# A gated stream of 64-row tiles: the first tile as two compact pieces, the larger stored first

## The chip, the cores and the metric

One core of one Trainium2 chip. The metric is device microseconds of one execution; medians of several runs are given with their range.

## The reference, cut to what matters

```python
# x: (1, 384, 384, 384) bfloat16; w1d: (1,) bfloat16
g = jnp.einsum("bhwc->bc", x) / (H * W)      # mean of every channel over 147456 pixels
s = _sigmoid(g * w1d[0])                     # k = 1: one weight
return x * s[:, None, None, :]               # every pixel times the gate of its channel
```

The gate depends on all of x, so read strictly, x would have to be read twice. The input is 113 MB; the kernel holds four tiles of 6.29 MB at a time.

## The kernel before

It guesses the gate from the first few pixels (`s_early`), multiplies and stores with that, sums everything on the way, and compares at the end the true gate with the guess, bit for bit in bfloat16. Only if a channel differs does a second pass run. So in the usual case x is read once and written once. A tile is 64 rows; a row is one pixel in each of 128 partitions, 768 bytes per partition. Four slots of 64 rows lie in SBUF. Loads go through the SP queue (some early ones through the ACT queue), stores through the ACT queue.

```python
TILE, SLOTS, EARLY, LEAD, FORE, OWN = 64, 4, 4, 8, 32, 16
PAUSE = 9
...
    def dram(view, r0, n):                    # n rows for each of 128 partitions, compact in HBM
        return view[r0 * P : (r0 + n) * P, :].rearrange("(p t) c -> p (t c)", p=P)
...
    def load(place, n, r0, queues=("sync",), lo=0, hi=None, reads=()):
        i, hi = lo, hi or n
        for queue, m in zip(queues, split(hi - lo, -(-(hi - lo) // len(queues)))):
            plan.dma(queue, at(place + i, m), dram(x_rows, r0, n)[:, i * C : (i + m) * C],
                     reads=reads, writes=rows(place + i, m))
            i += m
...
    def put(place, n, r0, to=None, parts=None):
        to, i = place if to is None else to, 0
        for m in parts or [n]:                # tile 0: two gate multiplies of 32 rows
            plan.op("vector", gate(to + i, place + i, m, s_early), ...)
            i += m
        plan.final.append(plan.dma("scalar", dram(o_rows, r0, n), at(to, n), reads=rows(to, n)))

    def pause(r0):                            # ScalarE writes row r0 of the slot: it has to wait
        to = at(base, PAUSE)                  # for the store that reads that row
        plan.op("scalar", ..., reads=["warm"], writes=rows(r0, 1) + ["pause"])
...
    load(0, TILE, 0, hi=LEAD)                                  # 8 of 64 rows: for the early gate
    plan.dma("sync", w_one[0:1, 0:1], w1d.unsqueeze(0), writes=["w_one"])
    load(0, TILE, 0, ("sync", "scalar"), lo=LEAD)              # the other 56, in two halves
    load(slot(1), TILE, row0(1))
    load(slot(2), TILE, row0(2), ("scalar", "scalar"))
    load(slot(3), TILE, row0(3))
...
    for k in range(n_tiles):
        if k >= SLOTS:
            for i in range(2) if k == SLOTS else () if k < SLOTS + 2 else (k - SLOTS,):
                sum_own(i)
                put(slot(i), TILE, row0(i), parts=None if i else (FORE, TILE - FORE))
            if k == SLOTS:
                pause(slot(k))
            load(slot(k), TILE, row0(k), reads=["pause"] if k == SLOTS else ())
```

The planner (not shown) turns reads and writes of rows into semaphore waits. The load of tile 4 goes into slot 0, so it waits for tile 0's store, and for the pause behind it.

Of the kernel before, what the change touches and what calls it, by code (L numbers as in the profile page):

```python
# [149 lines left out]
def split(n, most):  # L150
    k = -(-n // most)
    return [n // k + (i < n % k) for i in range(k)]
# [6 lines left out]
TILE, SLOTS, EARLY, LEAD, FORE, OWN = 64, 4, 4, 8, 32, 16  # L159
# [5 lines left out]
def bass_standalone__channel_attn_eca__vision_kernel(  # L165
# [8 lines left out]
    x_rows, o_rows = x.flatten_outer_dims(), out.flatten_outer_dims()  # L174

    def dram(view, r0, n):
        return view[r0 * P : (r0 + n) * P, :].rearrange("(p t) c -> p (t c)", p=P)

    ones = nc.alloc_sbuf_tensor("ones", [P, P], BF16)
    s_early = nc.alloc_sbuf_tensor("s_early", [P, C], BF16)  # L180
# [19 lines left out]
    def at(r0, n):  # L200
        assert r0 + n <= n_arena
        return arena[:, r0 * C : (r0 + n) * C]

    def rows(r0, n):
        return [("sb", r) for r in range(r0, r0 + n)]

    def gate(to, place, n, s):
        s_b = s[:].unsqueeze(1).broadcast_to([P, n, C])
        v, to_v = (at(r, n).rearrange("p (t c) -> p t c", t=n) for r in (place, to))
        return lambda e: e.tensor_tensor(to_v, v, s_b, ALU.mult)  # L210

    n_tiles = n_rows // TILE
# [3 lines left out]
    last = n_tiles - 1  # L216
    ready = nc.alloc_semaphore("ready")

    def slot(k):
        return k % SLOTS * TILE  # L220

    def row0(k):
        return k * TILE
# [2 lines left out]
    s_true = at(slot(last), 1)  # L226
    plan = Planner(nc, "a", 70)

    def load(place, n, r0, queues=("sync",), lo=0, hi=None, reads=()):

        i, hi = lo, hi or n
        for queue, m in zip(queues, split(hi - lo, -(-(hi - lo) // len(queues)))):
            plan.dma(
                queue,
                at(place + i, m),
                dram(x_rows, r0, n)[:, i * C : (i + m) * C],
                reads=reads,
                writes=rows(place + i, m),
            )
            i += m  # L240
# [90 lines left out]
    def sum_own(k):  # L331

        r0 = slot(k) + TILE - OWN
        view = at(r0, OWN).rearrange("p (t c) -> p c t", t=OWN)
        to = part if k else own
        plan.op(
            "vector",
            lambda e: e.reduce_sum(to[:], view, axis=mybir.AxisListType.X),  # L338
            reads=rows(r0, OWN),
            writes=["part" if k else "own"],  # L340
        )
        if k:
            plan.op(
                "vector",
                lambda e: e.tensor_tensor(own[:], own[:], part[:], ALU.add),  # L345
                reads=["own", "part"],
                writes=["own"],
            )
# [28 lines left out]
                writes=["acc_own"],  # L377
            )

    def put(place, n, r0, to=None, parts=None):  # L380
        to, i = place if to is None else to, 0
        for m in parts or [n]:
            plan.op(
                "vector",
                gate(to + i, place + i, m, s_early),
                reads=["s_early"] + rows(place + i, m),
                writes=rows(to + i, m),
            )
            i += m
        plan.final.append(  # L390
            plan.dma("scalar", dram(o_rows, r0, n), at(to, n), reads=rows(to, n))
        )

    def pause(r0):

        to = at(base, PAUSE)
        plan.op(
            "scalar",
            lambda e: e.activation(  # L399
                to, warm[:, 0:1].broadcast_to([P, PAUSE * C]), ACT_F.Sigmoid  # L400
            ),
            reads=["warm"],
            writes=rows(r0, 1) + ["pause"],
        )

    def weight():
# [25 lines left out]
    plan.op("gpsimd", lambda e: e.memset(warm[:, 0:1], 0.0), writes=["warm"])  # L432
    plan.op("vector", lambda e: e.memset(ones[:], 1.0), writes=["ones"])  # L433
    plan.op("gpsimd", lambda e: e.memset(zeros[:], 0.0), writes=["zeros"])
    load(0, TILE, 0, hi=LEAD)
    plan.dma("sync", w_one[0:1, 0:1], w1d.unsqueeze(0), writes=["w_one"])
    load(0, TILE, 0, ("sync", "scalar"), lo=LEAD)
    load(slot(1), TILE, row0(1))

    load(slot(2), TILE, row0(2), ("scalar", "scalar"))  # L440
# [10 lines left out]
        reads=["total", "w_scaled0", "warm1"],  # L451
        writes=["s_early"],
# [4 lines left out]
    for k in range(n_tiles):  # L457
        if k >= SLOTS:

            for i in range(2) if k == SLOTS else () if k < SLOTS + 2 else (k - SLOTS,):  # L460
                sum_own(i)
                put(slot(i), TILE, row0(i), parts=None if i else (FORE, TILE - FORE))
            if k == SLOTS:
                pause(slot(k))
            load(slot(k), TILE, row0(k), reads=["pause"] if k == SLOTS else ())
        there = rows(slot(k), TILE)
        plan.relay(ready, "gpsimd", "tensor", there, rows(slot(k), FORE), ["acc1"])
        plan.signals("tensor", rows(slot(k) + FORE, TILE - OWN - FORE), ["acc1"])
    plan.signals("tensor", [], ["acc1"])
    for k in range(n_tiles - SLOTS, last):  # L470
        sum_own(k)
        put(slot(k), TILE, row0(k))

    put(slot(last), TILE, row0(last), slot(n_tiles))
    sum_own(last)
    join_own()

# [5 lines left out]
        reads=["acc_own", "total"],  # L483
        writes=["total"],
# [6 lines left out]
        reads=["total", "w_scaled1"],  # L491
        writes=["s_true"] + rows(slot(last), 1),
# [6 lines left out]
        reads=["s_true", "s_early"],  # L499
        writes=["total"],  # L500
# [4 lines left out]
        reads=["total"],  # L505
        writes=["wrong"],
# [4 lines left out]
        reads=["wrong"],  # L511
        writes=["redo"],
# [6 lines left out]
    half, r0 = (base - above) // 2, 0  # L519
    for k, n in enumerate(split(n_rows, half)):  # L520
        place = above + k % 2 * half
# [4 lines left out]
            reads=rows(place, n),  # L526
            writes=rows(place, n),
# [98 lines left out]
```

## Time and profile before

| | before |
|---|---|
| median of 3 runs | 528.14 us (528.01 to 528.21) |
| span of the profiled run | 526.5 us |
| moved | 113.25 MB in, 113.25 MB out |
| DMA rate from 140 to 440 us | 435 GB/s |

From the timeline (start, length, engine, what), tile 0's and tile 1's store issues, and the pause:

```profile
44.14 24.76 ACTq L109 DMA_DIRECT2D out_dram<-arena  x2
76.09 3.08 ACT L399 ACTIVATE arena<-warm 128x3456 bf16<-128x3456 f32 x1 [61.87 <-DMA out_dram<-arena]
```

Two short stretches (the last column is GB/s):

```profile
1.00:10.00 9.00, 0.72 (x3) 0.20 (x2) 0.39 (x3) 1.49 (x2) 0.13 (x2) 1.00 1.02 395
50.00:57.00 7.00, 7.00 (x34) 0.00 (x0) 6.97 (x3) 0.00 (x0) 0.00 (x0) 1.00 0.98 390
```

(A stretch counts a packet whole where it starts, so stretches this short are coarse; with each packet's bytes spread over its time, the single records give 378 and 398 GB/s here.)

### The profile page before, as it was taken

What the parts mean: (1) busy time and instruction counts of PE and PEld (TensorE: products, weight loads), DVE (VectorE), ACT (ScalarE), POOL (GpSimd) and SP (SyncE); (2) the same over time, 40 slices, a digit from 0 to 9 for tenths busy, and PEclk for the clock granted to TensorE, in tenths of its full rate; (3) what the DMA queues carried; (4) which work ended last, traced back from release to release, by engine and by line L of the source; (5) the groups of instructions that cost most, each with busy time, mean ns of one, the idle gap of its engine ahead of it and who ended that gap; (6) DMA issues with size and microseconds to landing.
All of it is one profiled execution on the core that took longest, in us unless ns stands there. A gap on an engine that the chain in (4) does not pass through costs nothing.

```text
span 526.5 us, 902 instructions
## 1 busy us (share of the span) xinstructions
PE 180.0 (34%) x648; PEld 0.2 (0%) x2; DVE 440.0 (84%) x78; ACT 5.8 (1%) x5; POOL 0.3 (0%) x6
## 2 busy tenths in 40 slices
PE   2255752043240707061422506070513315070701
PEld 0000000000000000000000000000000000000000
DVE  1869999999996978969696969789696969698795
ACT  1000020000000000000000000000000000000000
POOL 0000000000000000000000000000000000000000
PEclk9996967558585858567575858576675858585765
DMA  9999999999999999999999999999999999999998
GB/s 375 433 459 405 418 448 448 418 418 467 429 418 418 467 429 418 429 459 426 418 429 459 426 418 441 445 429 418 448 437 429 418 459 429 426 418 459 429 426 359
DMA packets 5620, 226.51 MB, mean 430 GB/s; under 512 B 626, under 2 KB 626, under 8 KB 754
## 3 DMA queue, kind: packets, MB, share of 16 engines
q10 hardware_dynamic: 3024, 122.29, 53.7%
q1 hardware_dynamic: 2594, 104.20, 46.0%
q14 instruction: 2, 0.02, 0.0%
HBM read 113.25 MB, written 113.25 MB: 430 GB/s over the span
## 4 chain that ended last, share of the span: by engine, by line
DMA 42%; another core or an unknown queue 27%; DVE 21%; issue 7%; SPq 0%; ACT 0%; DVEq 0%
DMA arena<-in_x_dram 24%; DMA out_dram<-arena 18%; DVE part L338 12%; DVE arena L210 7%; DVE own L345 1%; DVE total L326 0%; SPq L109 0%; DVE own L363 0%; DVE terms L356 0%; ACT arena L488 0%; DVE total L496 0%; DVE total L482 0%; DVE wrong L504 0%; DVE total L324 0%
## 5 line engine op out<-in xcount | busy, mean ns | idle before, releaser
L248 PE MATMUL acc<-arena,ones 128*128 128x512 bf16 x637 | 176.1, 441 | 312.2 <-PEq L292 310.8
L210 DVE TENSOR_TENSOR arena<-arena,s_early 128x24576 bf16<-128x24576 bf16 (+1 forms) x19 | 233.2, 12278 | 11.5 <-PE acc L248 6.5
L338 DVE TENSOR_REDUCE part<-arena 128x384 f32<-128x6144 bf16 x17 | 179.2, 10539 | 56.9 <-DMA arena<-in_x_dram 56.9
L338 DVE TENSOR_REDUCE own<-arena 128x384 f32<-128x6144 bf16 x1 | 10.4, 10435 | 0.6 <-DMA arena<-in_x_dram 0.6
L345 DVE TENSOR_TENSOR own<-own,part 128x384 f32<-128x384 f32 x17 | 9.5, 558 | 0.6
L425 DVE TENSOR_SCALAR w_scaled<-w_all 128x1 f32<-128x1 f32 x2 | 0.2, 152 | 8.0 <-PE w_all L416 8.0
L248 PE MATMUL acc_own<-terms,ones 128*128 128x384 bf16 x3 | 1.4, 479 | 15.3 <-DVE terms L356 15.3
L488 ACT ACTIVATE arena<-total,w_scaled 128x384 bf16<-128x384 f32 x1 | 0.6, 615 | 440.3 <-DVE total L482 440.3
L326 DVE TENSOR_TENSOR total<-total,acc 128x128 f32<-128x128 f32 (+2 forms) x10 | 3.9, 393 | 0.3
L399 ACT ACTIVATE arena<-warm 128x3456 bf16<-128x3456 f32 x1 | 3.1, 3082 | 61.9 <-DMA out_dram<-arena 61.9
L416 PE MATMUL w_all<-w_one,ones 1*128 1x1 bf16 x1 | 0.2, 158 | 9.3 <-DMA w_one<-in_w1d_dram 9.3
L248 PE MATMUL acc<-zeros,ones 128*128 128x512 bf16 x6 | 2.3, 507 | 0.0
L324 DVE COPY total<-acc 128x384 f32<-128x384 f32 x2 | 1.1, 554 | 1.2 <-PE acc L248 1.2
L410 ACT ACT_TABLE_LOAD x1 | 1.3, 1283 | 2.3 <-issue 2.3
L433 DVE MEMSET ones<- 128x128 bf16 x1 | 0.2, 165 | 1.3 <-PEq L611 1.3
L363 DVE TENSOR_TENSOR own<-own,terms 128x384 f32<-128x384 f32 x2 | 1.1, 559 | 0.1
L356 DVE CAST terms<-own 128x384 bf16<-128x384 f32 x3 | 1.1, 359 | 0.1
L496 DVE TENSOR_TENSOR total<-arena,s_early 128x384 f32<-128x384 uint16 x1 | 0.6, 558 | 0.7 <-ACT arena L488 0.7
L448 ACT ACTIVATE s_early<-total,w_scaled 128x384 bf16<-128x384 f32 x1 | 0.6, 614 | 9.8 <-DVE total L326 9.8
L482 DVE TENSOR_TENSOR total<-total,acc_own 128x384 f32<-128x384 f32 x1 | 0.6, 554 | 0.1
L246 PE MATMUL acc<-arena,ones 128*128 128x512 bf16 x1 | 0.6, 608 | 0.0
L504 DVE TENSOR_REDUCE wrong<-total 128x1 f32<-128x384 f32 x1 | 0.6, 553 | 0.0
(10 smaller groups left out, 1.2 us busy)
## 6 DMA issues: line engine op xcount, KB each, us to landing
out_dram<-arena ACTq DMA_DIRECT2D x18, 6144.0 KB, 49.9
arena<-in_x_dram SPq DMA_DIRECT2D x16, 6144.0 KB, 41.8
arena<-in_x_dram ACTq DMA_DIRECT2D x2, 3072.0 KB, 41.5
arena<-in_x_dram ACTq DMA_DIRECT2D x1, 2688.0 KB, 14.0
arena<-in_x_dram SPq DMA_DIRECT2D x1, 2688.0 KB, 21.4
arena<-in_x_dram SPq DMA_DIRECT2D x1, 768.0 KB, 7.8
w_one<-in_w1d_dram SPq DMA_DIRECT2D x1, 0.0 KB
```

The costliest lines, as they stand in the source:

```text
L210: return lambda e: e.tensor_tensor(to_v, v, s_b, ALU.mult)
L246: loaded.append(e.matmul(bank, weights, moving, start=start, stop=stop))
L248: return e.add_instruction(mybir.InstMatmult(name=nc.get_next_instruction_name(), engine=mybir.EngineType.PE, ins=[e.lower_ap(moving), e.l ...
L324: emit = lambda e, part=part, of=of: e.tensor_copy(part, of)
L326: emit = lambda e, part=part, of=of: e.tensor_tensor(part, part, of, ALU.add)
L338: lambda e: e.reduce_sum(to[:], view, axis=mybir.AxisListType.X),
L345: lambda e: e.tensor_tensor(own[:], own[:], part[:], ALU.add),
L356: lambda e, term=term: e.tensor_copy(term, own[:]),
L363: lambda e, term=term: e.tensor_tensor(own[:], own[:], term, ALU.subtract),
L399: lambda e: e.activation(to, warm[:, 0:1].broadcast_to([P, PAUSE * C]), ACT_F.Sigmoid),
L410: lambda e: e.activation(warm[:, 1:2], warm[:, 0:1], ACT_F.Sigmoid),
L448: lambda e: e.activation(s_early[:], total[:], ACT_F.Sigmoid, scale=w_scaled[:, 0:1]),
```

## The change

Before, the first 8 rows of each partition were cut out of that partition's 64 rows, 49152 bytes from one partition to the next in HBM. Now the first tile is two compact blocks: 8 rows per partition (1024 pixels in a row in HBM), and 56 rows per partition behind them. Each is loaded by itself, and so each must be stored by itself; the larger goes first. The two gate multiplies of 32 rows stay. The rest of the diff is renaming.

```diff
--- before.py
+++ after.py
@@ -226,10 +226,10 @@
     s_true = at(slot(last), 1)
     plan = Planner(nc, "a", 70)
 
-    def load(place, n, r0, queues=("sync",), lo=0, hi=None, reads=()):
-
-        i, hi = lo, hi or n
-        for queue, m in zip(queues, split(hi - lo, -(-(hi - lo) // len(queues)))):
+    def load(place, n, r0, queues=("sync",), reads=()):
+
+        i = 0
+        for queue, m in zip(queues, split(n, -(-n // len(queues)))):
             plan.dma(
                 queue,
                 at(place + i, m),
@@ -377,19 +377,30 @@
                 writes=["acc_own"],
             )
 
-    def put(place, n, r0, to=None, parts=None):
-        to, i = place if to is None else to, 0
-        for m in parts or [n]:
-            plan.op(
-                "vector",
-                gate(to + i, place + i, m, s_early),
-                reads=["s_early"] + rows(place + i, m),
-                writes=rows(to + i, m),
-            )
-            i += m
+    def gated(place, n, to):
+        plan.op(
+            "vector",
+            gate(to, place, n, s_early),
+            reads=["s_early"] + rows(place, n),
+            writes=rows(to, n),
+        )
+
+    def store(place, n, r0):
         plan.final.append(
-            plan.dma("scalar", dram(o_rows, r0, n), at(to, n), reads=rows(to, n))
-        )
+            plan.dma("scalar", dram(o_rows, r0, n), at(place, n), reads=rows(place, n))
+        )
+
+    def put(k, to=None):
+        to = slot(k) if to is None else to
+        gated(slot(k), TILE, to)
+        store(to, TILE, row0(k))
+
+    def put_first():
+
+        gated(0, FORE, 0)
+        gated(FORE, TILE - FORE, FORE)
+        store(LEAD, TILE - LEAD, LEAD)
+        store(0, LEAD, 0)
 
     def pause(r0):
 
@@ -432,9 +443,9 @@
     plan.op("gpsimd", lambda e: e.memset(warm[:, 0:1], 0.0), writes=["warm"])
     plan.op("vector", lambda e: e.memset(ones[:], 1.0), writes=["ones"])
     plan.op("gpsimd", lambda e: e.memset(zeros[:], 0.0), writes=["zeros"])
-    load(0, TILE, 0, hi=LEAD)
+    load(0, LEAD, 0)
     plan.dma("sync", w_one[0:1, 0:1], w1d.unsqueeze(0), writes=["w_one"])
-    load(0, TILE, 0, ("sync", "scalar"), lo=LEAD)
+    load(LEAD, TILE - LEAD, LEAD, ("sync", "scalar"))
     load(slot(1), TILE, row0(1))
 
     load(slot(2), TILE, row0(2), ("scalar", "scalar"))
@@ -459,7 +470,7 @@
 
             for i in range(2) if k == SLOTS else () if k < SLOTS + 2 else (k - SLOTS,):
                 sum_own(i)
-                put(slot(i), TILE, row0(i), parts=None if i else (FORE, TILE - FORE))
+                put(i) if i else put_first()
             if k == SLOTS:
                 pause(slot(k))
             load(slot(k), TILE, row0(k), reads=["pause"] if k == SLOTS else ())
@@ -469,9 +480,9 @@
     plan.signals("tensor", [], ["acc1"])
     for k in range(n_tiles - SLOTS, last):
         sum_own(k)
-        put(slot(k), TILE, row0(k))
-
-    put(slot(last), TILE, row0(last), slot(n_tiles))
+        put(k)
+
+    put(last, slot(n_tiles))
     sum_own(last)
     join_own()
 
```

## The prediction

> **What bounds the kernel now.** I read the page first, for the busy shares.
>
> ```profile
> span 526.5 us, 902 instructions
> PE 180.0 (34%) x648; PEld 0.2 (0%) x2; DVE 440.0 (84%) x78; ACT 5.8 (1%) x5; POOL 0.3 (0%) x6
> DMA  9999999999999999999999999999999999999998
> HBM read 113.25 MB, written 113.25 MB: 430 GB/s over the span
> ```
>
> The reader is to see that no compute engine is full (the busiest, VectorE, has 84%), but that the DMA row is at nine tenths or more in all slices except the last. Every byte of x is read once and written once. The page averages stages, so next I cut the span into stretches; the last two columns are the DMA share and GB/s.
>
> ```profile
> 0.00:45.00 45.00, 13.99 (x44) 0.20 (x2) 26.89 (x13) 2.10 (x3) 0.33 (x6) 0.93 0.99 418
> 45.00:80.00 35.00, 24.94 (x97) 0.00 (x0) 34.93 (x6) 3.08 (x1) 0.00 (x0) 0.80 1.01 428
> 140.00:440.00 300.00, 105.88 (x383) 0.00 (x0) 248.13 (x32) 0.00 (x0) 0.00 (x0) 0.68 1.00 435
> 490.00:526.50 36.50, 11.23 (x41) 0.00 (x0) 30.20 (x18) 0.61 (x1) 0.00 (x0) 0.64 0.95 410
> ```
>
> From 45 to 490 us there is nothing to fill: the share is 0.99 to 1.01. Only the first microsecond (nothing in flight) and the last two (the final completion) are below it. The waits say the same from the other side. First VectorE and ScalarE, then the queue of the loads:
>
> ```profile
> ACT arena L399 <- DMA out_dram<-arena: 61.9, 1, 61.9
> DVE part L338 <- DMA arena<-in_x_dram: 56.9, 13, 5.3
> DVE arena L210 <- PE acc L248: 6.5, 1, 6.5
> ...
> SPq L109 <- DMA out_dram<-arena: 364.1, 13, 28.8
> ```
>
> VectorE waits for loads thirteen times; the issuer of the loads waits for stores to free a slot, thirteen times, about 28 us each. The chain of waits in order of time shows the beat in its middle (start, length, what):
>
> ```profile
> 215.76 0.33 SPq L109
> 216.09 28.71 another core or an unknown queue
> 244.80 0.02 issue
> 244.82 0.33 SPq L109
> 245.14 28.60 another core or an unknown queue
> ```
>
> One tile per about 28.95 us: two transfers of 6.29 MB in that time are 434.6 GB/s, the rate of the stretches. So this is a kernel bound by the DMA engines' time, with two queues (loads and stores) that keep each other company; the long waits in the chain are the queues' depth and not gaps.
>
> Because of that I worked out a floor from the trace's single packet records. One packet is one partition's row of a transfer: 49152 B take 1.815 us (4352 of them, nearly constant), 24576 B 0.912 us, 21504 B 0.799 us, 6144 B 0.234 us. Each of the 16 engines carries 8 partitions of each transfer: 34 whole-tile transfers give 272 x 1.815 = 493.7; the two halves of tile 2 give 16 x 0.912 = 14.6; the two 28-row pieces give 16 x 0.799 = 12.8; the 8-row piece gives 8 x 0.234 = 1.9; some 39 completion writes of 0.009 us make 0.4. Sum 523.4 us. The first packet starts at 1.0 us and the last data end at about 524.7 us, so over the whole run each engine is idle for about 0.3 us. The span is 1.0 + 523.4 + 0.3 + 1.8 (from the last data to the end).
>
> **What the Trainium skill says.** (1) The page "DMA: Bandwidth & Descriptors", section "Specifications", gives 435 GB/s as the ceiling of the 16 engines together; the trace agrees: 435 GB/s in the stretch from 140 to 440 us. (2) The same page, "Queues, rings and completion order", says that each engine goes round-robin between the queues that have work, one packet at a time. The trace agrees where both queues are full:
>
> ```profile
> DMA packets 2987, 130.36 MB, mean 435 GB/s; under 512 B 334, under 2 KB 334, under 8 KB 334
> q1 hardware_dynamic: 1500, 65.18, 50.2%
> q10 hardware_dynamic: 1486, 65.18, 50.2%
> ```
>
> Packet for packet, equal sizes, equal bytes. This is what makes packet size matter for who finishes first. (3) The same page, "Why small descriptors are slow (HBM only)", says that a packet has a small fixed overhead. The trace agrees in kind: from 49152 and 6144 B the slope is 1.581 us / 43008 B = 0.03676 ns per byte, and 0.234 us less 6144 of these leaves 8 ns per packet. (4) The same page, "Anatomy of one DMA", puts most of a fixed cost of about 2 us on the confirmation of the last write; here 1.8 us lie between the last data and the end, which agrees.
>
> **The change part by part.** All compute instructions are the same in number, size and order: VectorE still makes two gate multiplies of 32 rows (6.55 us each) for tile 0, and TensorE still sums the same rows. What moves is this.
>
> (a) Layout. Before, the 8-row piece was cut out of 64-row partitions, so neighbouring partitions' pieces lay 49152 B apart in the input; now the 8-row piece is one compact block and the other block has 56 rows per partition, loaded as two times 28. The packets are as before: 128 of 6144 B, 256 of 21504 B. Cost 0, if the place in HBM does not matter. The compute gets different pixels in its early estimate: 512 pixels out of the first 1024, in place of the first 8192.
>
> (b) The store of tile 0: 8 packets of 49152 B per engine become 8 of 43008 B and 8 of 6144 B. By the slope above 43008 B take an estimated 0.234 + 36864 x 0.03676/1000 = 1.589 us. Per engine: 8 x (1.589 + 0.234 - 1.815) = +0.064 us, plus one completion write, 0.009: +0.07 us, all of it on the bound resource.
>
> (c) One more issue on ScalarE's queue, about 0.34 us by the rows of the issues (0.338 median). It comes at 44.5 us, and the next store is not issued until 68.5 us; hidden.
>
> (d) The release of slot 0. The pause (ScalarE, 3.08 us, from 76.09 us) and behind it the load of tile 4 now wait for the small piece, which stands behind the big one. Here I worked by turns. At 44 us the load queue has 5.55 MB left, all of tile 3: 7.1 packets per engine. The store queue still has about 2.7 packets of tile 2's second half ahead of the store. These take 2.7 x (1.815 + 0.912) = 7.4 us, to 51.4, and leave 4.4 load packets. Before: 4.4 turns of 1.815 + 1.815 = 16.0, to 67.4; the load queue is empty; 3.6 store packets alone, 6.5, to 73.9; the trace has the landing at 76.07, so 2.1 of confirmation. After: 4.4 turns of 1.815 + 1.589 = 15.0, to 66.4; 3.6 x 1.589 = 5.7, to 72.1; eight small packets alone, 1.9, to 74.0; landing at about 76.1. So the release stays within 0.1 us, and tile 3 lands a microsecond earlier, which is worth nothing: VectorE comes to tile 3 only at 92.3 us.
>
> Sum: +0.07 us of DMA time, everything else hidden. 528.14 + 0.07 gives 528.2 us.
>
> **The rivals.** First, the small piece starves behind turns: if the load of tile 3 were still running, each 6144 B packet would be followed by a 49152 B one, 8 x (0.234 + 1.815) = 16.4 us in place of 1.9, and slot 0 would be released up to 14.5 us late. For it speaks the round-robin; against it the sum in (d), where the load runs dry some 6 us before, and that the bytes are the same: the engines would be fed by tile 1's store (alone 8 x 1.815 = 14.5 us from 74 us, to 88.5) and idle at most until the next store is issued at 92.4. It would make at most 528 + 4 = 532 us, still within 2%.
>
> Second, the place in HBM matters: the compact 8-row block is read by all engines at once. If its packets were twice as slow, 8 x 0.234 = 1.9 us more, 530 us. The first packets are already slow, up to 1.47 us, as the queues start. The delay of the early gate itself is hidden: it is ready at 14.2 us, and VectorE, after its first reduction (to 24.6), waits for TensorE until 31.08 anyway (the 6.5 us line above). In the other direction, a quicker start can give back at most about half a microsecond to 1 us.
>
> Third, the early gate differs from the true one and the whole second pass runs, another 226 MB, to about 1050 us. I computed it from the reference's inputs: the weight is 0.00123, the largest early mean 0.0067 with the new pixels (0.0065 with the old), so the gate is 0.5 within 2.1e-6 in all channels, far below half a bf16 step there (about 0.001). It rounds to 0.5 early and late. I hold this for excluded.
>
> Fourth, a real gain: 2% are 10.6 us, but only about 3 us of the span are not DMA work. Packets would have to become quicker. I see nothing that would do it.
>
> Fifth, the phase of loads against stores shifts, and the end with it. The last load lands at 489.9 us, its gate ends at 502.9, and the stores queued before it last to about 510: 7 us of slack. A shift of a microsecond costs nothing.
>
> **Range and chances.** The runs before lie within 0.2 us; the known change is 0.07; the unknowns (start, phase) are each half a microsecond, the rivals of 2 to 4 us unlikely. So 528.2 us, 8 in 10 between 527.3 and 529.3. Faster by over 2% 0.01, within 2% 0.975, slower by over 2% 0.015, the last mostly for an effect that I don't see.
>
> **What would show it.** In the profile after: DMA still at nines throughout; 128 more data packets under 8 KB (and 16 completion writes), so about 5,764 packets; 435 GB/s from 140 to 440 us; the pause starting at 76 us, within half a microsecond; the load queue dry a microsecond earlier than before, at about 67 to 68; the first landing at about 7.8 us; the last load at about 490 us. Wrong would be: the pause starting at 80 us or later (first rival), the first piece landing a microsecond or more later (second), a second pass of loads (third), or a stretch in the middle below 430 GB/s, which I have no reason for.

## More of the kernel before

From the page, transfers with their size and the median time from issue to landing:

```profile
out_dram<-arena ACTq DMA_DIRECT2D x18, 6144.0 KB, 49.9
arena<-in_x_dram SPq DMA_DIRECT2D x1, 768.0 KB, 7.8
```

## The result

The changed kernel took 528.65 us (median of 6 runs, 528.27 to 529.67), the kernel before 528.17 us (6 runs, 527.87 to 529.19). The ratio is 1.0009 with a 95% interval of 0.9996 to 1.0022. A ratio here is the mean time of one kernel's fast runs over the mean of the other's in the same rounds, so not quite the ratio of the medians. Run again with five rounds, it was 0.9997 (0.9984 to 1.0011).

The profile after, first the page, then the stretches that the prediction showed of before:

```profile
span 527.1 us, 905 instructions
DMA packets 5765, 226.51 MB, mean 430 GB/s; under 512 B 643, under 2 KB 643, under 8 KB 899
HBM read 113.25 MB, written 113.25 MB: 430 GB/s over the span
```

```profile
0.00:45.00 45.00, 14.23 (x46) 0.20 (x2) 27.60 (x13) 2.10 (x3) 0.33 (x6) 0.91 0.98 419
45.00:80.00 35.00, 23.94 (x91) 0.00 (x0) 34.93 (x6) 2.86 (x1) 0.00 (x0) 0.77 1.02 423
140.00:440.00 300.00, 108.51 (x378) 0.00 (x0) 247.39 (x31) 0.00 (x0) 0.00 (x0) 0.68 1.00 434
490.00:526.50 36.50, 11.69 (x41) 0.00 (x0) 30.28 (x18) 0.61 (x1) 0.00 (x0) 0.64 0.95 412
```

There are 128 more packets under 8 KB besides the completion writes, as foretold; each byte is still moved once, so there is no second pass; the middle runs at 434 GB/s. One row differs by more than 2 GB/s: 45 to 80 us has 423 in place of 428. That is the stretch with tile 0's store. Its lines from the timeline and from the transfers:

```profile
42.95 25.23 ACTq L109 DMA_DIRECT2D out_dram<-arena  x3
77.14 3.08 ACT L410 ACTIVATE arena<-warm 128x3456 bf16<-128x3456 f32 x1 [63.64 <-DMA out_dram<-arena]
```

```profile
out_dram<-arena ACTq DMA_DIRECT2D x1, 5376.0 KB, 32.3
arena<-in_x_dram SPq DMA_DIRECT2D x1, 768.0 KB, 7.7
out_dram<-arena ACTq DMA_DIRECT2D x1, 768.0 KB, 33.8
```

The small piece lands behind the large one, and the pause starts at 77.14 us, 1.05 us later than before, although the stores were issued 1.2 us sooner. The two short stretches:

```profile
1.00:10.00 9.00, 1.43 (x5) 0.20 (x2) 0.39 (x3) 1.49 (x2) 0.13 (x2) 1.00 1.04 417
50.00:57.00 7.00, 6.57 (x32) 0.00 (x0) 6.97 (x3) 0.00 (x0) 0.00 (x0) 1.00 0.96 340
```

The start is quicker than before (417 against 395 GB/s; 393 against 378 with the bytes spread over time), the joining of the first store slower (340 against 390; 352 against 398). The reader sees two effects of opposite sign where the prediction had written "cost 0, if the place in HBM does not matter".

The trace's single packet records put a size on both. I call a packet slow if it took over 60 ns more than the usual time for its size (1.815, 1.589, 0.912, 0.799 or 0.234 us), and add up the excess, divided by 16 engines. This table is worked out from those records, those of the loads and stores alone; it is no view of the profile:

```
profile of                       excess us per engine       packet time   last data
                           before 10   45 to 65   after 65   per engine    packet ends
before                        0.91       0.56       0.06       524.97        525.92
before, second profile        0.75       0.63       0.18       525.01        526.09
old layout, split store       0.80       0.76       0.13       525.23        526.40
old layout, all split         0.77       0.61       8.53       534.77        536.42
after                         0.49       1.29       0.08       525.39        526.57
after, second profile         0.53       1.36       0.10       525.52        526.68
after, release 3.1 us late    0.42       1.23       0.31       525.52        526.96
after, release 9.2 us late    0.43       1.35       3.11       528.52        532.43
after, no pause               0.28       1.30       0.24       525.32        528.32
8 rows first                  0.50       0.94       0.52       525.51        528.54
8 rows first, again           0.50       1.01       0.34       525.40        528.80
8 first, pause held           0.48       0.93       0.04       524.97        526.17
8 first, held, again          0.48       0.89       0.16       525.08        526.61
```

### The profile page after: what moved, and what is told of

Same layout as the page of the kernel before. It is cut to its first block, busy times and chain, and to the rows that moved or that the text cites. A ratio compares the mean times of both kernels' runs of the same rounds, so it can differ in the third digit from the quotient of the medians.

```text
span 527.1 us, 905 instructions
## 1 busy us (share of the span) xinstructions
PE 185.0 (35%) x648; PEld 0.2 (0%) x2; DVE 440.0 (83%) x78; ACT 5.8 (1%) x5; POOL 0.3 (0%) x6
## 2 busy tenths in 40 slices
DMA packets 5765, 226.51 MB, mean 430 GB/s; under 512 B 643, under 2 KB 643, under 8 KB 899
## 3 DMA queue, kind: packets, MB, share of 16 engines
HBM read 113.25 MB, written 113.25 MB: 430 GB/s over the span
## 4 chain that ended last, share of the span: by engine, by line
DMA 43%; another core or an unknown queue 27%; DVE 21%; issue 7%; SPq 0%; ACT 0%; DVEq 0%
DMA arena<-in_x_dram 24%; DMA out_dram<-arena 19%; DVE part L338 12%; DVE arena L210 7%; DVE own L345 1%; DVE total L326 0%; SPq L109 0%; DVE own L363 0%; DVE terms L356 0%; ACT arena L499 0%; DVE total L507 0%; DVE wrong L515 0%; DVE total L493 0%; DVE total L324 0%
## 5 line engine op out<-in xcount | busy, mean ns | idle before, releaser
L248 PE MATMUL acc<-arena,ones 128*128 128x512 bf16 x637 | 181.2, 451 | 309.0 <-PEq L292 307.4
L246 PE MATMUL acc<-arena,ones 128*128 128x512 bf16 x1 | 0.6, 609 | 0.0
## 6 DMA issues: line engine op xcount, KB each, us to landing
arena<-in_x_dram SPq DMA_DIRECT2D x16, 6144.0 KB, 41.8
```

The source lines that it names most:

```text
L246: loaded.append(e.matmul(bank, weights, moving, start=start, stop=stop))
L248: return e.add_instruction(mybir.InstMatmult(name=nc.get_next_instruction_name(), engine=mybir.EngineType.PE, ins=[e.lower_ap(moving), e.l ...
```

## The experiments

The theory to be tested: the DMA engines' packet time is the only thing that counts, and the change adds 0.07 us to it. The rivals: the place in HBM matters; the small piece is starved behind turns and the late release of slot 0 costs time; the phase of loads against stores moves the end; the early gate fails.

**1. The kernel before, against itself.** No edit.

> The kernel before, unchanged, run against itself: what differs is noise. Every theory expects a ratio of 1.000 with an interval of about 0.002 to either side. Its second profile tells how much the slow load packets beside the first store (near 53 us; they added 0.56 us per engine in the first profile of before, and 1.30 us in that of after) vary by themselves: if this profile shows 1 us or more, the 0.5 us between the two medians is chance; if it again shows about 0.5 us, the difference may belong to the change.

Measured: 528.08 us (median of 4), beside 528.37; ratio 1.0014 (0.9981 to 1.0046), with single runs up to 531.75 and 531.45. A difference of half a microsecond between medians can't be told from this spread. The second profile shows 0.63 us of slow packets near 53 us, again about half of the changed kernel's. The later profiles bear it out: 0.56 to 0.76 us in the four with the old layout, 1.23 to 1.36 us in the five of the table with the new one and the larger piece first. That part is not chance.

**2. The changed kernel again.** No edit, five rounds.

> The changed kernel, unchanged, with five rounds. If only packet time counts (theory: 0.07 us more work on the DMA engines and nothing else), the ratio is 1.0001 and lies within 0.001 of 1. If the change itself costs the 0.5 us that the first medians showed, the ratio is 1.0009 again and the profile shows again about 1.3 us per engine of slow load packets near 53 us.

Measured: 528.43 us (528.22 to 528.67), ratio 0.9997 (0.9984 to 1.0011). The time is that of before within the spread. The slow packets near 53 us are there again, 1.36 us. So the half microsecond of the first comparison is not shown as a difference in time, but a repeatable difference of 0.6 to 0.8 us lies inside, partly paid back at the start (0.51 in place of 0.83 us, means of two profiles each).

**3. The split store without the new layout.**

```diff
-        plan.final.append(
-            plan.dma("scalar", dram(o_rows, r0, n), at(to, n), reads=rows(to, n))
-        )
+        for lo, hi in ((LEAD, n), (0, LEAD)) if parts else ((0, n),):
+            plan.final.append(
+                plan.dma(
+                    "scalar",
+                    dram(o_rows, r0, n)[:, lo * C : hi * C],
+                    at(to + lo, hi - lo),
+                    reads=rows(to + lo, hi - lo),
+                )
+            )
```

> The layout of the kernel before (rows of 64 per partition), but tile 0 is stored in two strided pieces, 56 rows and behind it 8. The part of the change that costs packets, without the part that changes places in HBM. Theory (packets only): same as after, +0.07 us, ratio 1.000 within 0.001, pause at 76 to 77 us. Rival (place in HBM matters): this is equal to before and after is not. Rival (the first store of a different packet size makes the start of the stores dearer): slow load packets near 53 us as in after, about 1.3 us per engine.

Measured: 528.42 us (528.18 to 528.98), ratio 1.0001 (0.9987 to 1.0015). The pause starts at 76.16 us. Its two short stretches:

```profile
1.00:10.00 9.00, 0.84 (x3) 0.20 (x2) 0.39 (x3) 1.49 (x2) 0.13 (x2) 1.00 1.02 398
50.00:57.00 7.00, 7.00 (x33) 0.00 (x0) 6.96 (x3) 0.00 (x0) 0.00 (x0) 1.00 1.02 392
```

These are the numbers of before (395 and 390), not of after (417 and 340). So splitting the store into 56 and 8 rows costs nothing that a run can see, and the release moves by 0.1 us (76.09 and 76.02 us in the two profiles of before), as worked out. Both deviations of after come with the layout. At the start nothing else differs, so there it is the place in HBM. At the first store one thing more does: with the new layout the store was also issued 1.2 us sooner, and no run separates this from the place in HBM.

**4. The small piece first.**

```diff
-        store(LEAD, TILE - LEAD, LEAD)
         store(0, LEAD, 0)
+        store(LEAD, TILE - LEAD, LEAD)
```

> The changed kernel with the order of the two stores reversed: 8 rows first, 56 behind. By the turns of the queues the small packets now alternate with load packets (0.234 + 1.815 us per turn), so tile 3's load should have its last data at about 61 to 62 us in place of 70, while the 56-row store ends when the pair ended before, at 75 to 77 us. The pause starts with the small landing and so before the big one, by then at 68.5 us (it stands behind the second tile's store in its queue), and no longer delays the load of tile 4, which is issued at about 76 us in place of 80. Theory (work conserved): time within 0.5 us of after, ratio 1.000. Rival (the phase of loads against stores, or the release, sets the end): several us of difference in either direction, above 531 or below 526.

Measured: 530.23 us (530.04 to 531.47), ratio 1.0037 (1.0023 to 1.0052). Tile 3's load had its last data at 62.3 us in place of 70.6, the 56-row store ended at 76.1 us, and the load of tile 4 was issued at 76.55 us: the turns are as worked out. But the time is 1.8 us above after, neither "within 0.5 us" nor "above 531". Its last stretch, beside the same of experiment 5:

```profile
490.00:528.90 38.90, 12.01 (x41) 0.00 (x0) 30.29 (x18) 0.61 (x1) 0.00 (x0) 0.63 0.90 388
```

```profile
490.00:526.70 36.70, 12.50 (x41) 0.00 (x0) 30.30 (x18) 0.61 (x1) 0.00 (x0) 0.64 0.94 407
```

The packet time per engine is 525.51 us, the same as in after (525.52), yet the last data end 1.9 us later. I laid the packets end to end into 16 rows, which the records allow as each engine is without gaps (this is an inference; a record doesn't name its engine): fifteen engines end by 526.6 us, one at 528.54 us. The end is that of the slowest engine, not of the mean. The same rows tell more: the late one has as many packets as the others (264 of 49152 bytes, 8 of 43008), but 3.9 us of excess in slow packets after 65 us, where the other fifteen have 0.3 us on average.

**5. The small piece first, the pause held for both.** This makes the load of tile 4 wait until about 80 us again and keeps the order.

```diff
-            writes=rows(r0, 1) + ["pause"],
+            writes=rows(r0, LEAD + 1) + ["pause"],
```

> The reversed order again, but the pause now waits for both stores of tile 0, so that the load of tile 4 is issued at about 80 us as in after, not at 76.55 us. The reversed order alone took 530.23 us against 528.43 us of after. If its 1.8 us came from the missing pause, this is 528.4 us within 0.6. If they came from the order itself (small packets ahead of the big ones), this is 530.2 us within 0.6.

Measured: 528.19 us (528.11 to 528.72), ratio 1.0001 (0.9986 to 1.0016). The load of tile 4 is issued at 79.64 us. So the order alone, with the load held, costs nothing that a run can see.

**6. No pause, the order of the change.**

```diff
-            if k == SLOTS:
-                pause(slot(k))
-            load(slot(k), TILE, row0(k), reads=["pause"] if k == SLOTS else ())
+            load(slot(k), TILE, row0(k))
```

> The changed kernel without the pause: the load of tile 4 is issued when tile 0's store has landed, at about 77.5 us and not at 80.6 us. If the missing pause cost the reversed order its 1.8 us, this is 530 us or more. If the order itself cost them, this is 528.4 us within 0.6.

Measured: 528.57 us (528.2 to 530.19), ratio 1.0004 (0.9989 to 1.0019), load of tile 4 at 77.02 us. Five runs of six lie at 528.2 to 528.9; the sixth, which is the profiled one, took 530.19 us, and there again one engine ends alone, at 528.32 us, the others by 526.2. So neither the order nor the missing pause by itself makes 1.8 us in the median.

**7. and 8. Experiments 4 and 5 again, on one chip,** because they had run on two.

> The reversed order without a working pause once more, beside its held version on the same chip, because the two ran on different chips before. If the 1.8 us belong to the kernel, this is again about 1.5 to 2 us above the held version, and in its profile again one DMA engine ends 2 us or more behind the others. If they belonged to the chip, both are equal within 0.6 us.

> The reversed order with the pause held for both stores: 528.2 us within 0.6, as on the other chip, if the held pause is what keeps the engines together.

Measured: 530.37 us for the order without a working pause, with runs at 528.39, 528.40 and four from 530.20 to 531.13; 528.21 us with the pause held, five runs at 528.02 to 528.47 and one at 530.61. (The ratios to before, 1.0016 and 0.9995, have intervals of 0.003, since a run of before took 532.74 us.) In the profile of the first, one engine ends at 528.80, the next at 526.66 us. The 1.8 us belong to the kernel and not to the chip, but not to every run: there are two outcomes, about 2 us apart. 9 of 11 runs of the reversed order with the early load took over 530 us, 1 of 6 with the early load alone (experiment 6), 1 of 12 with the order reversed and the load held, 4 of 42 of before, and none of 11 of after. So in these runs it took the order and the early load together to make the longer outcome common, but the kernel before has it too (if by the same cause, no profile shows). In all three profiles that end late (experiments 4, 6 and 7) the late row of packets has the same work as the others and 3.1 to 3.9 us of its own in slow packets after 65 us, nearly all of them loads and many of them about 29 us, one tile, apart; the mean of the other rows is 0.05 to 0.3 us. One engine's packets run slow; why that engine's do, and why this is common with the reversed order and the early load, stays open.

**9. The release of slot 0 made 9.2 us late.**

```diff
-                pause(slot(k))
+                for _ in range(4):
+                    pause(slot(k))
```

> The changed kernel with the pause repeated four times: the release of slot 0 is 9.2 us later, the load of tile 4 issued at about 89.8 us in place of 80.6 us. This does to the release what the first rival feared, in size. Theory (work conserved): in these 9.2 us tile 1's store (8 packets of 1.815 us per engine, from about 75.6 to 90 us) keeps the engines busy, so no time is lost in the middle; the last load lands some 4 to 9 us later than the 490 us of before, within the 9 us that the queued stores leave: 528.4 us, at most 530. Rival (a late release costs what it is late, or half of it): 533 to 538 us.

Measured: 532.58 us (532.30 to 537.17), ratio 1.0092 (1.0068 to 1.0117). The load of tile 4 was issued at 89.88 us, as meant. Against before on this chip that is 4.6 us for a load of tile 4 that is 10.7 us later (79.19 us in before's profile), against after's 528.43 us on another chip 4.1 us for 9.2. My expectation of at most 530 us fell. The rival's "533 to 538" was missed by 0.4 us as a median, and two of the six runs (536.0 and 537.17 us) lie in it: somewhat under half of the lateness was paid in the median. In the profile (of the run with 537.17 us, the longest) packets are slow again, 3.11 us per engine after 65 us, the densest part (1.3 us) at 91 to 96 us, where the loads start again and the next store joins them; the last load lands at 502.0 us, and the check on VectorE ends late:

```profile
502.00 12.96 DVE L210 TENSOR_TENSOR arena<-arena,s_early 128x24576 bf16<-128x24576 bf16 x1 [5.00 <-DMA arena<-in_x_dram]
533.37 0.15 DVE L522 CAST redo<-wrong 128x1 int32<-128x1 f32 x1
```

The last data end at 532.43 us and the span is 535.7 us: in that run the check is what ends last, not the last store. In the runs of 532.4 us no profile tells which of the two it is.

**10. The release made 3.1 us late,** with the pause twice.

> The changed kernel with the pause made twice: the release is 3.1 us later than in after, which had it 1.0 to 1.5 us later than before. If the last check on VectorE has about 2.8 us of slack (last load landing at 489.9 us, its chain 31.5 us, 2.2 us to the end: 523.6 of 526.4 us) and a late release moves the last load by as much, this is 528.6 to 529.4 us. If half of any lateness is paid, 530 us. If nothing is paid, 528.4 us.

Measured: 529.27 us (529.07 to 529.47), ratio 1.0008 (0.9977 to 1.0038), within the first expectation. The check ends at 525.3 us; before it ended at 521.4 us. From the chain of before and of this kernel:

```profile
521.28 0.15 DVE redo L510
```

```profile
525.17 0.15 DVE redo L522
```

The load of tile 4 was issued at 83.15 us, 4.0 us later than in before (79.19), and the last load and the check came 3.9 us later, so the lateness is passed on in full. The time grew by under 1 us (0.8 against after's 528.43 us, across two chips). In experiment 9, 2.2 us lay between the check and the end of the span; with those the check would end this run at 527.5 of its 527.8 us, so its slack is used up here. That the span ends 0.8 us behind the last data packet, and only 0.4 to 0.55 us in the other profiles of the table but experiment 9's, fits this. A release that is late by 1.0 to 1.5 us, as in after, lies within the slack: its check ended at 522.1 and 522.2 us of 527.1 and 527.2.

**11. Every store split in 56 and 8 rows.** The edit of experiment 3 without its condition: 18 small pieces amid loads in full flow.

> The kernel before, but every tile's store is two strided pieces, 56 rows and behind it 8, so that 18 small pieces have to take turns with loads in full flow: 8 turns of 0.234 + 1.815 us. Theory (work conserved, 0.073 us more per split store): 528.1 + 18 x 0.073 = 529.4 us, ratio 1.002; the engines stay busy and the loads get more of each turn. Rival (starvation: each store lands 14.5 us later, and since load 42, compute 24 and store 50 us close a circle over four slots, 116 us = 4 x 29, the circle grows to 130 us, 32.6 us per tile): 528 + 14 x 3.6 = about 578 us.

Measured: 538.28 us (537.36 to 539.31), ratio 1.0193 (1.0173 to 1.0213), verdict "unclear" as 2% lies in the interval; that it is slower by about 10 us is clear. Neither 529.4 nor 578. Landings and the middle stretch:

```profile
arena<-in_x_dram SPq DMA_DIRECT2D x16, 6144.0 KB, 28.8
out_dram<-arena ACTq DMA_DIRECT2D x18, 5376.0 KB, 57.3
out_dram<-arena ACTq DMA_DIRECT2D x18, 768.0 KB, 62.6
```

```profile
140.00:440.00 300.00, 99.84 (x367) 0.00 (x0) 247.91 (x31) 0.00 (x0) 0.00 (x0) 0.68 1.00 423
```

The small pieces do give turns away: a load now lands in 28.8 us in place of 41.8, a tile's store in 62.6 in place of 49.9. The circle doesn't grow by the difference, as what the store loses the load gains. The engines are never idle (share 1.00), so "work conserved" holds as to gaps, but the rate is 423 in place of 435 GB/s: packets became slower. Packet time per engine grew by 9.8 us (534.77 less 525.0); 18 x 0.073 = 1.3 us is the overhead of the additional packets, and the table has 8.5 us of slow packets after 65 us. They are nearly all loads of 49152 bytes, 8.0 us of the 8.5. With the packets laid end to end as in experiment 4, 6.5 us of these 8.0 fall on loads that have two packets of one queue in a row among the last five up to and with them, that is where turns start or stop, and 1.5 us on the other, about as many, loads. But in the kernel before as many loads stand so, with 0.05 us in all; the change of turns alone is not the cause. What makes those packets slow stays open: the pieces are small, they are written apart from each other in HBM, and the loads run dry during each, and no run separates these.

**12. The early gate made wrong,** so that the second pass runs; the result stays right, since that pass writes everything.

```diff
-            s_early[:], total[:], ACT_F.Sigmoid, scale=w_scaled[:, 0:1]
+            s_early[:], total[:], ACT_F.Sigmoid, scale=1.0
```

> The changed kernel with a wrong scale in the early gate, so that the comparison at the end fails and the second pass runs: the third rival's mechanism, forced. The result stays correct, as the second pass writes everything. It moves another 226.5 MB; at 430 to 435 GB/s that is 520 to 527 us more, some 1050 us in all. An unforced after shows no such pass.

Measured, one run of unknown state: 1081.93 us, correct.

```profile
span 1080.4 us, 970 instructions
HBM read 226.49 MB, written 226.49 MB: 419 GB/s over the span
```

A failed guess doubles the bytes, and the second pass is somewhat slower than the first (412 GB/s from 540 to 1060 us), so my 1050 us were 3% low (with one run of unknown state, no more can be said). After moved 113.25 MB each way: this rival didn't happen.

## Why the prediction was right or wrong

**Right, and in the main for the reason given.** The DMA engines' packet time sets the end, and the change hardly touches it. 528.2 us was said; the two comparisons gave 528.65 and 528.43 us, ratios 1.0009 and 0.9997. Some of it was luck: the layout, priced at nothing, had two effects that partly cancel, and the lateness of the release fell into a slack that the prediction had read off the wrong chain. Of the signs, 5,765 packets, the first landing at 7.7 us, 434 GB/s in the middle and the last load at 490.5 us came as said; the pause did not.

**Step (b), the price of the split store, was right.** 43008-byte packets took 1.589 us in every record of after and of experiment 3, the value interpolated; the split without the new layout (experiment 3) takes 1.0001 of before and moves the pause by 0.1 us.

**Step (a), the layout, was mis-sized.** "Cost 0, if the place in HBM does not matter": it does at the start, and the layout, by its place in HBM or by the earlier store that follows from it, does at the first store. At the start the compact block is quicker, 0.51 in place of 0.83 us of excess per engine. At the first store it is slower, 1.33 in place of 0.60 us (means of two profiles each). Net about 0.4 us per engine, where 0 was written; the times are too scattered to show it. Experiment 3 separates this from the split. The second rival had the place in HBM right as a cause, but looked for a loss at the start, where there is a gain, and not at the first store. Why the loads at the first store are slower after a compact first tile is not settled; the 8-rows-first kernels, with the same layout, have 0.9 to 1.0 us there, at about 59 us and not 53, so it depends on which store packets come first as well.

**Step (d), the release, was off by a microsecond.** The pause was to start within half a microsecond of 76 us and started at 77.14 and 77.55 us. The turns were counted wrong already for before: its store began at 55.2 to 55.8 us on 15 of the 16 engines (packets laid end to end), and on one alone at 51.3 us, the 51.4 of the sum; three loads, not 4.4, took turns with it. By their completion writes, the 16 engines ended the store at 75.13 to 75.72 us, not at 73.9, so the "2.1 of confirmation" that closed the sum was mostly the sum's own shortfall; the pause came 0.4 us behind the last data packet (75.7 us). The same shortfall stood in the sum for after, and so the difference of 0.1 us looked sound. What the sum lacked in the difference are the slow packets and the spread of the engines: in after the store's last completion writes came at 75.53 to 76.78 us, the earliest 0.4 us later than before and the latest 1.1 us, and a landing needs the latest. The loads ran dry sooner on 15 engines, as said, but by about 0.6 us (completion writes at 67.3 to 68.4 in place of 67.9 to 68.5 us); the sixteenth had its last load data at 70.0 us before and 70.2 after.

**The division of the span was wrong though its sum came out.** "1.0 + 523.4 + 0.3 + 1.8" took the usual time for every packet and called the rest confirmation. The records add up to 524.97 us per engine (1.5 us of it excess of slow packets), and the last data end at 525.92 us, on the slowest engine; about 0.5 us lie behind it, not 1.8.

**The slack at the end was taken from the wrong chain.** "7 us of slack" counted the last gate and the queue of stores. The check on VectorE has less: it ended at 521.4 us of 526.5. Experiments 9 and 10 show it: 3.1 us later than after cost under 1 us, 9.2 us later some 4. The change itself is late by 1.0 to 1.5 us and stays below that.

**The first rival was excluded rightly, but not for a reason that carries over.** In this change the small packets run when the loads are done, as (d) says. Where they don't (experiment 11), turns are given away but no time is lost by that, since the engines stay busy; slower packets make it dearer, 10.3 us for 18 pieces, some 0.6 us each.

**Open:** why the loads of one engine run slow in some runs, and what makes load packets slow where stores join. On most engines the slow load near 53 us is the one directly ahead of the store's first packet.

## What to carry to other kernels

Where the DMA engines are busy all the time, price a change in packets first: so many per engine by the recorded time for their size. One split store, priced at 0.07 us, cost too little here for a run to see. But don't stop there: eighteen cost 10.3 us where 1.3 were priced. Check the rate of busy engines in stretches of a few microseconds, above all where stores join loads: a busy share of 1.00 doesn't say that packets run at their usual pace, and splitting every store cost 10 us here with no idle engine to be seen. For the slack of the end, follow each chain that must finish, the check as well as the last store, and remember that a landing is that of the slowest of 16 engines.

## What the Trainium skill lacked or had wrong

- "DMA: Bandwidth & Descriptors", "Anatomy of one DMA": it breaks down a fixed cost of about 2 us, mostly the receipt of the last write, for DMAs issued by GpSimd alone, and gives no such figure for stores issued by ScalarE. Here the pause started 0.4 us after the last data packet of tile 0's store (75.7 to 76.09 us), and the span ended 0.5 us after the last data.
- "DMA: Bandwidth & Descriptors", "Queues, rings and completion order": round-robin by packets fits (with 56 + 8 split stores, loads landed in 28.8 in place of 41.8 us), but it has nothing of packets getting slower where a second queue starts or stops: 0.6 to 1.4 us per engine at the first store, and 8.5 us over the run with all stores split.
- The pages on DMA, HBM and SBUF have the pitch of rows in HBM as a matter of large powers of two only (512 KiB and up). Loading the first tile in compact pieces, with 6144 and 43008 in place of 49152 bytes from one partition to the next, lowered the excess of slow packets at the start from 0.83 to 0.51 us per engine; at the first store it went with a rise from 0.60 to 1.33 us.
- None of these pages has an engine that is late in some runs of a kernel only: one of 16 engines ended about 2 us behind the others with equal packets (528.54 us against 526.6), which made 530.2 of 528.4 us. "DMA: Bandwidth & Descriptors", "Latency and other measured facts", has two engines that are usually slower, without a figure, and ascribes this, as a best guess, to what GpSimd-issued DMAs do; the loads and stores here are issued by SyncE and ScalarE, and the records don't name the engine.
